# Clamp and low part of the first four weight chunks: from VectorE to Pool

## The chip, the cores and the metric

One Trainium2 chip, one core. The metric is the device time of one execution in microseconds (us). Times of before and after are medians over runs; a profile is one execution. Engines: TensorE is PE in the tables, VectorE is DVE, ScalarE is ACT, GpSimd is Pool; SP issues the DMAs.

## What is computed

An attention whose mask lets a query see the keys of its own cluster, then two layers of a feed-forward kind, each over 1536 tokens with d_model 512 and d_ff 2048:

```python
def _attn_ref(q, k, v, centroids):        # 2 x 8 heads, S = 768, D = 64
    q_assign = np.argmax(q_n . c_n); k_assign = np.argmax(k_n . c_n)
    mask = q_assign[:, :, :, None] == k_assign[:, :, None, :]
    scores = np.where(mask, scale * q @ k.T, -1000000000.0)
    attn = np.exp(scores - max) ; attn = attn / (sum + 1e-09)
    return attn @ v
def _moe_ref(x, w_in, w_out):
    h = x @ w_in
    g = h * np.cos(h)
    return (g @ w_out).astype(np.float32)
def _moe2_ref(x, w_in, w_out):
    h = x @ w_in
    g = np.where(h >= 1, h, np.where(h <= -1, 0.0, (h + 1) ** 2 / 4))
    return (g @ w_out).astype(np.float32)
```

(The lines of the attention are shortened; `...n` are normalised vectors.) The weights of the two layers lie in memory as 64-bit floating-point words.

## The kernel before

Matrix products are made of three matmuls each, since an operand is kept as a high part and a low part (names in h and l: xh, xl; gh, gl; phi, plo): high times high, low times high, high times low (lines 734 to 736).

**Weights.** Each layer's weights come in tiles of 512 columns, w_in and w_out by turns, and each tile as two chunks of 128 x 1024 words; 32 chunks in all. `convert_chunk(n)` turns a chunk into high and low part in seven instructions: Abs on ACT (line 144) into the tile wx, clamp on DVE (146), a shift with mask on DVE (148, below: shl), the low word or-ed in on DVE (151), the sign or-ed in on DVE (154, below: the sign step), the high part on Pool (160, hi), the low part on DVE as wx minus hi (163, lo). With hi, SP is told to load the next chunk. There is one wx and one buffer for the raw words, so a chunk's Abs waits for the lo of the chunk before. The code is a generator with six steps for a chunk, and `pump` takes the next step: in the attention at slots 69, 77, and so on up to 189 (one in eight), after that one with each h tile and each y tile of the layers. So chunk 0 has its Abs at slot 69, clamp at 77, shl at 85, lo at 109; chunk 1 its clamp at 125, lo at 157; chunk 2 its clamp at slot 173 and shl at 181; the rest of chunk 2 and chunk 3 come with the first two blocks of the first layer. Chunks 0 and 1 are the first w_in tile (w_0), chunks 2 and 3 the first w_out tile (w_1): the first y tile needs chunk 2 for f 0 and 1, chunk 3 for f 2 and 3.

**Attention.** 192 slots, 24 for a pair of heads. A slot makes scores (PE, lines 514 and 517); DVE takes the row maximum nm (523), ACT the exponential p (532) with its sum; PE turns p over in three transposes into pt (566), ACT copies it to phi (569), DVE makes plo (574); PE multiplies with the values (584, 585). Three buffers hold pt and the like, so a transpose waits until DVE has made the plo of an earlier one. Pool makes den (541) and rb (552), the values' parts (478, 479), th and tl (318, 319), and xt, xh, xl of a finished pair (606, 607, 623, 624).

**First layer.** For a block of 512 tokens and four f, PE makes an h tile of 12 matmuls; ACT rounds it to n (707), DVE reduces to r (708), ACT takes sine (709) and square (710), DVE makes g (713), Pool gh (696), DVE gl (700). Four buffers hold h, so the fifth h tile waits for the g of the first. Then y tiles of 12 matmuls over four f.

**What sets the order.** Slots 18 to 179 are issued under a manual schedule: PE, ACT, DVE and Pool take the instructions in the written order. Outside of it, from slot 180 on and for work that a step of a late slot issues, the framework's scheduler orders each engine.

Of the kernel before, what the change touches and what calls it, by code (L numbers as in the profile page):

```python
# [8 lines left out]
F32 = mybir.dt.float32  # L9
# [5 lines left out]
ALU = mybir.AluOpType  # L15
# [8 lines left out]
HIGH_MIN = 2.0 ** -15  # L24
HIGH_MAX = 122876.0
# [7 lines left out]
def attention_moe_moe(  # L33
# [18 lines left out]
    nc = tc.nc  # L52
# [76 lines left out]
    def issue_chunk(n):  # L129
        if n >= len(wchunks):  # L130
            return
        src, c0, _ = wchunks[n]
        raw = w0pool.tile([P, 2, 512], I64, tag="wraw", bufs=1, name=f"wraw{n}")
        nc.sync.dma_start(raw, src[:, c0:c0 + 2])
        wraw[n] = raw

    def convert_chunk(n):

        _, c0, w = wchunks[n]
        words = wraw.pop(n).bitcast(I32).rearrange("p c (f t) -> p c f t", t=2)  # L140
        low, high = words[:, :, :, 0], words[:, :, :, 1]
        x = w0pool.tile([P, 2, 512], F32, tag="wx", bufs=1, name=f"wx{n}")
        xi = x.bitcast(I32)
        nc.scalar.activation(x, high.bitcast(F32), AF.Abs)  # L144
        yield
        nc.vector.tensor_scalar(x, x, HIGH_MIN, HIGH_MAX, ALU.max, ALU.min)
        yield
        nc.vector.tensor_scalar(xi, xi, 3, 0x3FFFFFFF,
                                ALU.logical_shift_left, ALU.bitwise_and)
        yield  # L150
        nc.vector.scalar_tensor_tensor(xi, low, 29, xi,
                                       ALU.logical_shift_right, ALU.bitwise_or)
        yield
        nc.vector.scalar_tensor_tensor(xi, high, -0x40000000, xi,
                                       ALU.bitwise_and, ALU.bitwise_or)
        if not wslot:
            wslot.append(w0pool.tile([P, 2, 4, 512], F32R, tag="w_0", name="w_0"))
        t = wslot[w % 4]
        hi, lo = t[:, 0, c0:c0 + 2], t[:, 1, c0:c0 + 2]
        nc.gpsimd.tensor_scalar(hi, x, 1.0, 0.0, ALU.mult, ALU.add)  # L160
        issue_chunk(n + 1)
        yield
        nc.vector.tensor_tensor(lo, x, hi.bitcast(F32), ALU.subtract)
        yield

    for l, (wi, wo) in enumerate(((w1_in, w1_out), (w2_in, w2_out))):
# [7 lines left out]
    def weight_steps():  # L174
        for n in range(len(wchunks)):
            for _ in convert_chunk(n):
                yield n
# [646 lines left out]
```

## Time and profile before

| | us |
|---|---|
| median of 3 runs | 796.08 |
| lowest, highest | 795.78, 798.86 |
| profiled execution | 797.14 |
| its span | 795.2 |
| busy: PE, DVE, ACT, Pool | 774.2, 622.7, 404.0, 282.8 |

The profiled execution took 1.94 us more than its span, and 1.06 more than the median. Times in the rows below are counted from the span's start. A row of a timeline is a run of like instructions: start, duration, engine, line, operation, output and inputs, how often; a bracket gives the idle time of the engine before it and what ended it.

### The profile page before, as it was taken

What the parts mean: (1) busy time and instruction counts of PE and PEld (TensorE: products, weight loads), DVE (VectorE), ACT (ScalarE), POOL (GpSimd) and SP (SyncE); (2) the same over time, 40 slices, a digit from 0 to 9 for tenths busy, and PEclk for the clock granted to TensorE, in tenths of its full rate; (3) what the DMA queues carried; (4) which work ended last, traced back from release to release, by engine and by line L of the source; (5) the groups of instructions that cost most, each with busy time, mean ns of one, the idle gap of its engine ahead of it and who ended that gap; (6) DMA issues with size and microseconds to landing.
All of it is one profiled execution on the core that took longest, in us unless ns stands there. A gap on an engine that the chain in (4) does not pass through costs nothing.

```text
span 795.2 us, 11159 instructions
## 1 busy us (share of the span) xinstructions
PE 774.2 (97%) x3964; PEld 652.9 (82%) x3964; DVE 622.7 (78%) x945; ACT 404.0 (51%) x768; POOL 282.8 (36%) x428
## 2 busy tenths in 40 slices
PE   8899999999999999999999999999999999999998
PEld 5789888888888778888888888888788888888886
DVE  6878988989999597777888788898876988755552
ACT  3788888789788565543333434222444333222220
POOL 4358568578554532122222122342231122111110
PEclk9999999999999999999999999999999999999999
DMA  6864654664430111231311213122122122000012
GB/s 160 192 157 120 145 129 99 145 170 107 88 98 1 54 54 53 106 106 53 107 54 58 101 54 106 54 88 72 54 72 88 53 67 93 0 1 1 19 48 92
DMA packets 46390, 65.95 MB, mean 83 GB/s; under 512 B 27904, under 2 KB 30848, under 8 KB 46336
## 3 DMA queue, kind: packets, MB, share of 16 engines
q1 hardware_dynamic: 46192, 65.22, 29.2%
q8 instruction: 31, 0.51, 0.3%
q14 instruction: 23, 0.19, 0.1%
q10 hardware_dynamic: 144, 0.03, 0.0%
HBM read 43.02 MB, written 3.15 MB: 58 GB/s over the span
## 4 chain that ended last, share of the span: by engine, by line
PE 60%; DVE 22%; POOL 5%; ACT 5%; issue 5%; DMA 3%; SPq 0%; DVEq 0%; POOLq 0%; ACTq 0%
PE y L736 7%; PE y L734 7%; PE y L735 7%; PE pt L566 7%; PE h L734 6%; PE h L735 6%; PE h L736 6%; PE s L514 3%; PE s L517 3%; DVE gl L700 3%; PE o L585 2%; PE o L584 2%; POOL gh L696 2%; DVE plo L574 2%; DVE g L713 2%
## 5 line engine op out<-in xcount | busy, mean ns | idle before, releaser
L696 POOL TENSOR_SCALAR gh<-g 128x512 fp32r<-128x512 f32 x96 | 71.4, 745 | 273.3 <-DVE g L727 152.0
L734 PE MATMUL h<-xh,w 128*128 128x512 f32 x384 | 149.7, 390 | 1.3 <-DVE g L713 0.8
L735 PE MATMUL h<-xl,w 128*128 128x512 f32 x384 | 149.5, 389 | 0.0
L736 PE MATMUL h<-xh,w 128*128 128x512 f32 x384 | 149.4, 389 | 0.0
L569 ACT ACTIVATE phi<-pt 128x384 fp32r<-128x384 f32 x192 | 94.4, 495 | 25.5 <-PE pt L566 22.3
L523 DVE TENSOR_REDUCE nm<-s 128x1 f32<-128x768 f32 x96 | 91.2, 950 | 19.7 <-PE s L517 16.9
L566 PE MATMUL pt<-ident,p 128*128 128x128 f32 x576 | 96.7, 276 | 8.3 <-DVE plo L574 7.0
L574 DVE TENSOR_TENSOR plo<-pt,phi 128x384 fp32r<-128x384 f32 x192 | 98.4, 546 | 7.5 <-ACT phi L569 7.3
L723 ACT ACTIVATE p<-h,ones 128x512 f32<-128x512 f32 x48 | 33.1, 690 | 125.9 <-DVE m L722 125.5
L566 PEld LDWEIGHTS pt<-ident,p 128*128 128x128 f32 x576 | 69.8, 140 | 26.3 <-issue 4.9
L532 ACT ACTIVATE p<-s,nm 128x768 f32<-128x768 f32 x96 | 86.6, 902 | 7.7 <-DVE nm L523 6.1
L700 DVE TENSOR_TENSOR gl<-g,gh 128x512 fp32r<-128x512 f32 x96 | 72.4, 754 | 21.1 <-POOL gh L696 15.4
L734 PEld LDWEIGHTS h<-xh,w 128*128 128x128 f32 x384 | 72.1, 188 | 17.1 <-DVE g L713 1.2
L144 ACT ACTIVATE wx<-wraw 128x1024 f32<-128x1024 f32 x32 | 36.4, 1137 | 96.1 <-DMA wraw<-in_moe_w_out_dram 47.4
L735 PEld LDWEIGHTS h<-xl,w 128*128 128x128 f32 x384 | 72.1, 188 | 14.9
L736 PEld LDWEIGHTS h<-xh,w 128*128 128x128 f32 x384 | 72.1, 188 | 14.8
L514 PE MATMUL s<-st,st 128*128 128x384 f32 x192 | 80.2, 418 | 2.6 <-ACT p L532 2.3
L734 PE MATMUL y<-gh,w 128*128 128x512 f32 x192 | 74.8, 390 | 1.6 <-POOL w L160 1.6
L735 PE MATMUL y<-gl,w 128*128 128x512 f32 x192 | 74.7, 389 | 0.0
L734 PE MATMUL y<-w,gh 128*128 128x512 f32 x192 | 74.7, 389 | 0.0
L735 PE MATMUL y<-w,gh 128*128 128x512 f32 x192 | 74.7, 389 | 0.0
L736 PE MATMUL y<-w,gl 128*128 128x512 f32 x192 | 74.7, 389 | 0.0
(129 smaller groups left out, 1548.2 us busy)
## 6 DMA issues: line engine op xcount, KB each, us to landing
wraw<-in_moe_w_in_dram SPq DMA_DIRECT2D x16, 1024.0 KB, 5.1
wraw<-in_moe_w_out_dram SPq DMA_DIRECT2D x16, 1024.0 KB, 4.8
st<-t SPq DMA_DIRECT2D x24, 192.0 KB, 4.2
st<-th SPq DMA_DIRECT2D x9, 384.0 KB, 4.0
st<-tl SPq DMA_DIRECT2D x18, 192.0 KB, 3.9
st<-th SPq DMA_DIRECT2D x18, 192.0 KB, 3.9
nat<-in_q_dram SPq DMA_DIRECT2D x8, 384.0 KB, 4.6
nat<-in_k_dram SPq DMA_DIRECT2D x8, 384.0 KB, 5.1
```

The lines of the kernel that those rows point to most:

```text
L144: nc.scalar.activation(x, high.bitcast(F32), AF.Abs)
L514: nc.tensor.matmul(s[:, step, :HS], qt[:, 0, cols], kt[:, 0, kc], start=True, stop=False)
L523: nc.vector.tensor_reduce(nm, s[:, :, :HS], AX.XY, ALU.max, negate=True)
L532: nc.scalar.activation(p, s[:, :, :HS], AF.Exp, bias=nm, accum_out=dens[u][:, jj, 0:1])
L566: nc.tensor.transpose(ps[:, jj * P:(jj + 1) * P], p[:, kt * P:(kt + 1) * P], ident)
L569: nc.scalar.activation(hi, ps, AF.Copy)
L574: nc.vector.tensor_tensor(lo, ps, hi.bitcast(F32), ALU.subtract)
L696: nc.gpsimd.tensor_scalar(hi, g, 1.0, 0.0, ALU.mult, ALU.add)
L700: nc.vector.tensor_tensor(lo, g, hi.bitcast(F32), ALU.subtract)
L734: nc.tensor.matmul(o, lh, rh, start=first, stop=False)
L735: nc.tensor.matmul(o, lh, rl, start=False, stop=False)
L736: nc.tensor.matmul(o, ll, rh, start=False, stop=last)
```

## The change

In `convert_chunk`, for the chunks 0 to 3 the clamp and the low part are issued on Pool instead of DVE. The other five instructions, the steps and the later 28 chunks are as before.

```diff
@@ -137,13 +137,14 @@
     def convert_chunk(n):
 
         _, c0, w = wchunks[n]
+        engine = nc.gpsimd if n < 4 else nc.vector
         words = wraw.pop(n).bitcast(I32).rearrange("p c (f t) -> p c f t", t=2)
...
-        nc.vector.tensor_scalar(x, x, HIGH_MIN, HIGH_MAX, ALU.max, ALU.min)
+        engine.tensor_scalar(x, x, HIGH_MIN, HIGH_MAX, ALU.max, ALU.min)
...
-        nc.vector.tensor_tensor(lo, x, hi.bitcast(F32), ALU.subtract)
+        engine.tensor_tensor(lo, x, hi.bitcast(F32), ALU.subtract)
         yield
```

From line 138 on the changed kernel's lines are one higher: clamp 147, shl 149, low word 152, sign step 155, hi 161, lo 164, plo 575. For chunks 0 and 1 the written order holds, and Pool has the clamp and lo where their slots stand. From slot 173 on the scheduler's order differs.

DVE round the clamp of chunk 2 (wx2), slots 171 to 175, before; nm90 and nm91 are row maxima, plo28_5 the low part of the last turned tile of unit 28:

```order
L618 TENSOR_TENSOR xt2_6_0_3773<-xt1_6_0_3727,r6_0_3828 128x384 [waits PE_49,Pool_49]
L523 TENSOR_REDUCE nm89_3844<-s89_3819 128x1 [waits PE_49]
L574 TENSOR_TENSOR plo28_3_3840<-pt28_3_3835,phi28_3_3839 128x384 [waits DVE_49,Activation_49]
L574 TENSOR_TENSOR plo28_4_3851<-pt28_4_3846,phi28_4_3850 128x384 [waits DVE_49,Activation_49]
L545 RECIPROCAL den28_3695<-den28_3695 128x3 [waits Pool_49]
L523 TENSOR_REDUCE nm90_3887<-s90_3853 128x1 [waits PE_49]
L146 TENSOR_SCALAR wx2_3740<-wx2_3740 128x1024
L574 TENSOR_TENSOR plo28_5_3873<-pt28_5_3868,phi28_5_3872 128x384 [waits DVE_49,Activation_49]
L574 TENSOR_TENSOR plo29_0_3895<-pt29_0_3890,phi29_0_3894 128x384 [waits DVE_49,Activation_49]
L523 TENSOR_REDUCE nm91_3918<-s91_3897 128x1 [waits PE_49]
L574 TENSOR_TENSOR plo29_1_3912<-pt29_1_3907,phi29_1_3911 128x384 [waits DVE_49,Activation_49]
```

The same place after:

```order
L524 TENSOR_REDUCE nm89_3844<-s89_3819 128x1 [waits PE_49]
L575 TENSOR_TENSOR plo28_3_3840<-pt28_3_3835,phi28_3_3839 128x384 [waits DVE_49,Activation_49]
L575 TENSOR_TENSOR plo28_4_3851<-pt28_4_3846,phi28_4_3850 128x384 [waits DVE_49,Activation_49]
L546 RECIPROCAL den28_3695<-den28_3695 128x3 [waits Pool_49]
L524 TENSOR_REDUCE nm90_3887<-s90_3853 128x1 [waits PE_49]
L575 TENSOR_TENSOR plo28_5_3873<-pt28_5_3868,phi28_5_3872 128x384 [waits DVE_49,Activation_49]
L575 TENSOR_TENSOR plo29_0_3895<-pt29_0_3890,phi29_0_3894 128x384 [waits DVE_49,Activation_49]
L149 TENSOR_SCALAR wx2_3740<-wx2_3740 128x1024 [waits Pool_49]
L524 TENSOR_REDUCE nm91_3918<-s91_3897 128x1 [waits PE_49]
L575 TENSOR_TENSOR plo29_1_3912<-pt29_1_3907,phi29_1_3911 128x384 [waits DVE_49,Activation_49]
```

The clamp is gone from behind nm90, and shl of wx2 stands behind plo29_0, waits for Pool, and has nm91 and plo29_1 behind it.

Pool at the same place, before; xh and xl are the parts of a finished pair's output:

```order
L606 TENSOR_SCALAR xt2_6_1_3879<-xt0_6_1_3633 64x384 [waits Pool_49]
L606 TENSOR_SCALAR xt2_6_1_3879<-xt1_6_1_3833 64x384 [waits Activation_49]
L606 TENSOR_SCALAR xt1_6_1_3833<-xt0_6_1_3633 64x384 [waits Pool_49]
L607 TENSOR_TENSOR xt1_6_1_3833<-xt1_6_1_3833,xt2_6_1_3879 128x384 [waits Pool_49]
L541 TENSOR_SCALAR den29_3796<-den29_3796 128x3 [waits Activation_49]
L552 TENSOR_SCALAR rb7_0_3885<-den28_3695 128x3x64 [waits DVE_49,PE_49]
L606 TENSOR_SCALAR xt2_7_0_4121<-xt0_7_0_3941 64x384 [waits Activation_49,Pool_49]
L623 TENSOR_SCALAR xh_103<-xt2_6_1_3879 128x384 [waits DVE_49,Pool_49]
```

And after:

```order
L607 TENSOR_SCALAR xt2_6_1_3879<-xt0_6_1_3633 64x384 [waits Pool_49]
L607 TENSOR_SCALAR xt2_6_1_3879<-xt1_6_1_3833 64x384 [waits Activation_49]
L607 TENSOR_SCALAR xt1_6_1_3833<-xt0_6_1_3633 64x384 [waits Pool_49]
L608 TENSOR_TENSOR xt1_6_1_3833<-xt1_6_1_3833,xt2_6_1_3879 128x384 [waits Pool_49]
L542 TENSOR_SCALAR den29_3796<-den29_3796 128x3 [waits Activation_49]
L553 TENSOR_SCALAR rb7_0_3885<-den28_3695 128x3x64 [waits DVE_49,PE_49]
L147 TENSOR_SCALAR wx2_3740<-wx2_3740 128x1024
L607 TENSOR_SCALAR xt2_7_0_4121<-xt0_7_0_3941 64x384 [waits Activation_49,Pool_49]
L624 TENSOR_SCALAR xh_103<-xt2_6_1_3879 128x384 [waits DVE_49,Pool_49]
```

The clamp of wx2 stands behind rb7_0, where xt2_7_0 stood.

PE at the first y tiles of the first layer, before; y0_0_0_0 and y0_0_0_1 are the first two of them, and w_1 is the weight tile of chunks 2 and 3:

```order
L734 MATMUL y0_0_0_0_4401<-gh0_0_0_4199,w_1_4193 128x512
L735 MATMUL y0_0_0_0_4401<-gl0_0_0_4200,w_1_4193 128x512
L736 MATMUL y0_0_0_0_4401<-gh0_0_0_4199,w_1_4193 128x512
L734 MATMUL y0_0_0_0_4401<-gh0_0_0_4199,w_1_4193 128x512
L735 MATMUL y0_0_0_0_4401<-gl0_0_0_4200,w_1_4193 128x512
L736 MATMUL y0_0_0_0_4401<-gh0_0_0_4199,w_1_4193 128x512
L734 MATMUL y0_0_0_1_4418<-gh0_0_0_4199,w_1_4193 128x512
L735 MATMUL y0_0_0_1_4418<-gl0_0_0_4200,w_1_4193 128x512
L736 MATMUL y0_0_0_1_4418<-gh0_0_0_4199,w_1_4193 128x512
L734 MATMUL y0_0_0_1_4418<-gh0_0_0_4199,w_1_4193 128x512
L735 MATMUL y0_0_0_1_4418<-gl0_0_0_4200,w_1_4193 128x512
L734 MATMUL y0_0_0_0_4401<-gh0_0_0_4199,w_1_4193 128x512
```

And after:

```order
L735 MATMUL y0_0_0_0_4401<-gh0_0_0_4199,w_1_4193 128x512
L736 MATMUL y0_0_0_0_4401<-gl0_0_0_4200,w_1_4193 128x512
L737 MATMUL y0_0_0_0_4401<-gh0_0_0_4199,w_1_4193 128x512
L735 MATMUL y0_0_0_0_4401<-gh0_0_0_4199,w_1_4193 128x512
L736 MATMUL y0_0_0_0_4401<-gl0_0_0_4200,w_1_4193 128x512
L737 MATMUL y0_0_0_0_4401<-gh0_0_0_4199,w_1_4193 128x512
L735 MATMUL y0_0_0_0_4401<-gh0_0_0_4199,w_1_4193 128x512
L736 MATMUL y0_0_0_0_4401<-gl0_0_0_4200,w_1_4193 128x512
L737 MATMUL y0_0_0_0_4401<-gh0_0_0_4199,w_1_4193 128x512
L735 MATMUL y0_0_0_0_4401<-gh0_0_0_4199,w_1_4193 128x512
L736 MATMUL y0_0_0_0_4401<-gl0_0_0_4200,w_1_4193 128x512
```

Before, the first six matmuls of y0_0_0_0 (f 0 and 1, chunk 2) are followed by five of y0_0_0_1, and the twelfth is the first that reads chunk 3. After, y0_0_0_0 goes through: its seventh matmul reads the high part of chunk 3, its ninth the low part. On DVE, in this layer, the sign step of chunk 3 stood behind the sixth r, the low word, both g, one gl and the seventh r; after, it stands right behind the sixth r, and the low word ahead of the third gl. On Pool lo of chunk 2 stands behind its hi and ahead of the first gh, the clamp of chunk 3 behind the first gh, its hi behind the fourth gh, and its lo behind the fifth. On ACT the first sine stands ahead of the second n, and the first square behind it; the Abs of chunk 3 stands behind the second sine, where it stood behind the second square and the third n. From about 545 us of the trace of before on, all orders are the same again.

## Rows read from the trace of the kernel before

**Rows 1.** The page: busy us and count by engine; chain's shares; the group of line 144.

```profile
PE 774.2 (97%) x3964; PEld 652.9 (82%) x3964; DVE 622.7 (78%) x945; ACT 404.0 (51%) x768; POOL 282.8 (36%) x428
...
PE 60%; DVE 22%; POOL 5%; ACT 5%; issue 5%; DMA 3%; SPq 0%; DVEq 0%; POOLq 0%; ACTq 0%
...
L144 ACT ACTIVATE wx<-wraw 128x1024 f32<-128x1024 f32 x32 | 36.4, 1137 | 96.1 <-DMA wraw<-in_moe_w_out_dram 47.4
```

**Rows 2.** Windows: from:to, length, busy us (count) of PE, PEld, DVE, ACT, Pool; clock, DMA.

```profile
170.00:250.00 80.00, 76.02 (x506) 68.83 (x506) 73.48 (x130) 67.92 (x150) 49.84 (x79) 1.00 0.42 104
...
300.00:560.00 260.00, 260.00 (x1149) 215.36 (x1148) 210.32 (x276) 100.19 (x156) 64.97 (x75) 1.00 0.23 77
```

**Rows 3.** Waits of PE, whole span: who for whom, us in total, times, longest.

```profile
PE pt L566 <- DVE plo L574: 7.0, 23, 0.8
```

**Rows 4.** Timeline of PE, at the gaps that the prediction names: start, us, instruction, [idle before].

```profile
168.59 0.52 PE L566 MATMUL pt<-ident,p 128*128 128x128 f32 x3 [0.71 <-DVE plo L574]
...
229.56 0.52 PE L566 MATMUL pt<-ident,p 128*128 128x128 f32 x3 [0.84 <-DVE plo L574]
...
249.75 0.52 PE L566 MATMUL pt<-ident,p 128*128 128x128 f32 x3 [0.24 <-DVE plo L574]
...
277.19 0.50 PE L734 MATMUL h<-xh,w 128*128 128x512 f32 x1 [0.77 <-DVE g L713]
...
290.48 0.39 PE L735 MATMUL y<-gl,w 128*128 128x512 f32 x1
...
292.47 0.50 PE L734 MATMUL y<-gh,w 128*128 128x512 f32 x1 [1.60 <-POOL w L160]
```

**Rows 5.** Groups of Pool by line and shape: busy us, mean ns, idle before.

```profile
L160 POOL TENSOR_SCALAR w<-wx 128x1024 fp32r<-128x1024 f32 x32 | 35.1, 1097 | 95.2 <-DVE wx L154 95.2
...
L607 POOL TENSOR_TENSOR xt<-xt,xt 128x384 f32<-128x384 f32 x16 | 16.5, 1034 | 1.3
...
L281 POOL TENSOR_TENSOR cn<-cn 64x64 f32<-64x64 f32 x2 | 0.6, 324 | 0.1
```

**Rows 6.** Timeline of DVE, at the conversion steps and their neighbours.

```profile
124.73 0.68 DVE L146 TENSOR_SCALAR wx<-wx 128x1024 f32<-128x1024 f32 x1
...
135.12 0.90 DVE L148 TENSOR_SCALAR wx<-wx 128x1024 int32<-128x1024 int32 x1
...
166.63 1.34 DVE L163 TENSOR_TENSOR w<-wx,w 128x1024 fp32r<-128x1024 f32 x1
...
246.40 0.95 DVE L146 TENSOR_SCALAR wx<-wx 128x1024 f32<-128x1024 f32 x1
...
247.27 0.54 DVE L574 TENSOR_TENSOR plo<-pt,phi 128x384 fp32r<-128x384 f32 x1
...
248.20 0.94 DVE L523 TENSOR_REDUCE nm<-s 128x1 f32<-128x768 f32 x1
...
276.45 0.69 DVE L713 SCALAR_TENSOR_TENSOR g<-r,h 128x512 f32<-128x512 f32 x1 [1.05 <-ACT r L710]
...
286.66 0.68 DVE L713 SCALAR_TENSOR_TENSOR g<-r,h 128x512 f32<-128x512 f32 x1
...
289.70 1.21 DVE L154 SCALAR_TENSOR_TENSOR wx<-wraw,wx 128x1024 int32<-128x1024 int32 x1
```

**Rows 7.** Timeline of Pool, in the attention part.

```profile
166.99 1.85 POOL L319 TENSOR_TENSOR tl<-t,th 128x384 fp32r<-128x384 f32 x1
...
176.96 1.01 POOL L457 TENSOR_TENSOR eq<-eq,desc 128x384 f32<-128x384 f32 x1 [3.54 <-PE s L517]
...
231.85 0.20 POOL L541 TENSOR_SCALAR den<-den 128x3 f32<-128x3 f32 x1 [3.97 <-ACT p L532]
...
243.41 0.52 POOL L623 TENSOR_SCALAR xh<-xt 128x384 fp32r<-128x384 f32 x1 [3.52 <-DVE xt L618]
...
246.89 1.33 POOL L607 TENSOR_TENSOR xt<-xt,xt 128x384 f32<-128x384 f32 x1
...
248.58 0.35 POOL L552 TENSOR_SCALAR rb<-den 128x192 f32<-128x192 f32 x1
```

## The prediction

> **What bounds the kernel now.** I read the busy shares first, then the windows by stage, the waits of PE, the timelines of PE round each gap, and last VectorE (DVE) and Pool beside these gaps. PE is busy 97% of the span [rows 1] and runs at full granted clock in the windows that matter, so only time in which PE stands still can be won. From 300 to 560 us PE is busy for all of the 260 us [rows 2]; what the change does to DVE and Pool there can only cost. It can win in two places. In the attention part DVE is the next limit: 73.48 of the 80 us between 170 and 250 [rows 2], and PE waits 23 times for plo of DVE, 7.0 us in all [rows 3]. At the start of the first MoE layer PE waits 0.77 us for g and 1.60 us for the high part of chunk 3 [rows 4]. Of the 7.0 us three gaps of PE lie right behind a conversion step that the change moves: 0.71 us at 168.59, 0.84 at 229.56 and 0.24 at 249.75 [rows 4]. All gaps that the change can touch sum to 4.2 us, half a per cent of the time.
>
> **The moved operations.** Eight instructions go from DVE to Pool, all 128x1024: four clamps and four subtractions (lo). On DVE they cost 0.68 and 1.34 us [rows 6]. Pool's clamp has the shape and the single tensor input of hi (line 160), which takes 1.10 us in the mean [rows 5]; I take 1.05, and as upper bound the price of a two-input operation, below. Pool never runs a two-input operation of this size. Its two-input forms take 0.324 us on 64x64 and 1.034 on 128x384 [rows 5]: (1.034 − 0.324) / 320 elements = 2.2 ns an element, so 1.034 + 640 × 2.2 ns = 2.4 us for 1024; in proportion it would be 1.034 × 1024 / 384 = 2.76. I take 2.4, the line through both forms. Below both there is little room, since the operation already costs 1.034 at 384.
>
> **Clamps of chunks 0 and 1: nothing.** DVE's clamp at 124.73 is followed by shl only at 135.12 [rows 6]: over 10 us in which Pool can do 1.05. No PE gap follows either clamp in the timeline. Pool's order there is the written one, and what it delays is th and tl of tiles that are needed later. Between 0 and −0.1 each; I take 0.
>
> **Low parts of chunks 0 and 1: −1.55.** DVE's lo at 166.63 (its row stands in [rows 6]; chunk 1's, at 227.56, is the like) is followed by the PE gaps of 0.71 and 0.84 us [rows 4]. Without lo DVE gives plo 1.3 us sooner, which is more than each gap. So both go: −0.71 − 0.84 = −1.55. On Pool, lo ends some 2.4 us after about 171.9 and 227.9; Pool then idled 3.54 us before 176.96 and 3.97 before 231.85 [rows 7], which hides it. The den and rb that chunk 0's lo pushes back are small and are wanted 5 us later or more. A gain could be smaller where ACT is next (then down to 0); it can't exceed the gaps.
>
> **Clamp of chunk 2: +2.15.** Here the order is the framework's, not the written one. Before, DVE did the clamp at 246.40 and shl much later; after, shl stands right behind plo29_0 and waits for Pool, and behind it are nm91, plo29_1 and all that PE needs next (order of DVE, first pair). On Pool the clamp stands behind the chain that began with xh at 243.41 and ended with rb at 248.58 + 0.35 = 248.93 [rows 7] (order of Pool, second pair). Of this chain 0.3 us came in at 246.89, where Pool's two-input step took 1.33 us [rows 7] against a mean of 1.03 [rows 5], beside DVE's clamp, which itself took 0.95 instead of 0.68 [rows 6]; without it the chain ends at 248.6, and the clamp runs from 248.7 to 249.7. DVE, without the clamp, is through nm90, plo28_5 and plo29_0 at 246.40 + 0.93 = 247.3 (their step is 248.20 − 247.27 [rows 6]) and then stands still for 2.4 us. shl takes 0.6 to 0.7 more (0.68 for the clamp of its shape at 124.73 [rows 6]), so nm91 starts at about 250.35 and not at 248.20 [rows 6]: 2.15 later. PE had no reserve: it waited for this plo already, 0.24 us at 249.75 [rows 4]. So PE resumes 2.15 us later, and that is the cost. Bounds: 0, if Pool's chain is 2.4 us sooner than I have it, and +3.5, if the clamp takes 2.4 us.
>
> **Low part of chunk 2, all of chunk 3: 0, between −0.8 and +0.8.** At the start of the MoE layer lo leaves DVE, and ACT's order lets the first sine and square go ahead of the second rounding. g of the first tile, at 276.45 before [rows 6], is then some 0.5 us sooner, and of PE's gap of 0.77 us at 277.19 [rows 4] about 0.5 goes. What follows is decided at y. A matmul's step is 260.00 / 1149 = 0.23 us [rows 2]. Before, PE did 11 matmuls of y, the last at 290.48, and resumed at 292.47 [rows 4]. After, y0_0_0_0 comes in one run (order of PE, third pair), whose ninth matmul needs the low part of chunk 3, so PE stands still after 8. On DVE the sign step of chunk 3 has lost the clamp and stands ahead of the four instructions between 286.66 and 289.70 [rows 6]: 289.70 − 0.5 − 3.04 − 0.6 = 285.6 with DVE unbroken, 286.5 if g of the second tile waits for most of the chunk's Abs on ACT (1.14 us [rows 1]), which I take. From there: 1.2 sign, 1.05 hi, 0.6 gh, 2.4 lo, to 291.8. Before, PE had 8 matmuls behind it when it had 3 × 0.23 = 0.68 fewer than at 292.47, so 291.79 is the like time: no difference. With DVE unbroken it is −0.8; with 2.76 for lo +0.4, and +0.8 if DVE holds it up for another half operation.
>
> First the row: beside DVE's lo at 166.63 Pool's subtraction of 128x384 took 1.85 us [rows 7] and not the 1.03 of the same shape in line 607 [rows 5]. The Trainium skill, "SBUF — State Buffer", section "Who interferes with whom", says that DVE and GpSimd share one pair of ports, that the one who issues first holds it for its whole instruction, and that a DVE instruction with two SBUF inputs is one that takes it. The trace agrees as far as these rows go. By that rule the sum would be higher by one such DVE instruction in Pool's way, and by rows alone it is as given; it is the upper part of rival C.
>
> **Sum.** −1.55 + 2.15 + 0 = +0.6 us. The profiled execution took 797.14 us, so 797.7; it lay 1.06 above the median of the three runs, and on the median the forecast is 796.08 + 0.6 = 796.7 us. About 0.5%, or 4 us, is what a measurement of this kernel can tell from no change, so this counts as no difference.
>
> **Rivals.**
> (B) DVE doesn't wait for the clamp of chunk 2. It needs Pool to reach it at 247.3, as when the chain from 243.41 starts sooner because DVE, freed of two lo, runs ahead. Against it: each link of that chain was back to back. Then only the gains stay, −1.55, perhaps with the 0.24 gap: 794.5.
> (C) Pool's subtraction is the slow one, and the restart of y pays. Place: the ninth matmul of y0_0_0_0, behind hi, gh and lo on Pool. It decides from about 2.4 us for lo on, one for one: at 2.76 it is +0.4, and with DVE in the way for 0.8 us, as at 166.99 (1.85 against 1.03 [rows 5, 7]), +1.2. With the other terms, 796.7 + 0.4 to 796.7 + 1.2, it is 797.1 to 797.9, and up to 798.7 if the clamp of chunk 2 is held by the same 0.8 us. For it: that row. Against it: the other two-input steps of Pool keep near 1.03 in the mean [rows 5]. The case ends 1.0 to 2.6 us above before.
> (D) The moved work changes nothing that PE sees: ACT gives the pace in attention, the gains of 1.55 don't come, and the DVE wait is taken up by PE's waits behind it, which are all short. 796.1, and up to 796.5.
> (E) The whole order of DVE in the first MoE layer is new, and opens PE gaps between 300 and 545 us, where there were none: DVE work there is 210 of 260 us [rows 2], so one gap of a moved step, 1.2 to 2.4 us, is its price: 798 to 799.
>
> **How the numbers follow.** Forecast, 795.9 to 797.4: 0.45. B, 794.0 to 795.5: 0.2. C, 797.4 to 798.7: 0.18. D: 0.07. E: 0.06. What is left, 0.04, lies outside on either side. The range of 794.3 to 799.2 takes in the forecast, D, most of B and of C and E, 8 in 10 or a little more. A faster kernel by over 0.5% (under 792.1) would need all touched gaps gone and more: 0.03. Slower by over 0.5% (over 800.06) needs C and E together or a longer DVE wait: 0.06. Within 0.5%: 0.91.
>
> **What would show it.** In the profile after, PE's gaps at 168.6 and 229.6 are gone. DVE idles some 2.4 us ahead of line 149 near 247.3 with Pool's wx of line 147 as releaser, and PE has a gap of about 2.4 us for plo near 250. Pool's line 164 takes about 2.4 us four times, line 147 about 1.05. PE waits at y for Pool's w of line 164, not 161, and resumes within 0.8 us of before. From 300 us on PE has no new gap. I am wrong if DVE doesn't wait there (B), if line 164 takes 2.8 us or more (C), or if PE waits in the h and y stages behind 300 us (E).

## The result and the profile after

The changed kernel takes 806.24 us in the median of 4 runs (805.93 to 806.67); the kernel before took 796.14 beside it. The ratio is 1.0124, with a 95% interval of 1.0112 to 1.0136: some 10 us slower. The forecast was 796.7, with a range of 794.3 to 799.2; a kernel slower by over 0.5% had a chance of 0.06.

The page of after (busy us and count by engine), against [rows 1]:

```profile
PE 777.6 (97%) x3963; PEld 655.0 (81%) x3964; DVE 617.7 (77%) x937; ACT 402.4 (50%) x768; POOL 303.9 (38%) x436
```

PE's own work grew by 3.4 us though it does the same matmuls; the rest of the loss is idle time. The waits of PE (us in total, times, longest), against [rows 3]:

```profile
PE pt L567 <- DVE plo L575: 10.9, 21, 5.2
...
PE y L737 <- POOL w L164: 2.2, 1, 2.2
...
PE h L735 <- DVE g L714: 1.9, 2, 1.7
```

Before, the waits for plo were 23, none over 0.8 us. Now one of 5.2 us is among 21. The wait for g at h has grown to 1.9, and y waits for the low part of line 164. What Pool does in the moved instructions, by line and shape (busy us, mean ns, idle before), against [rows 5]:

```profile
L161 POOL TENSOR_SCALAR w<-wx 128x1024 fp32r<-128x1024 f32 x32 | 34.7, 1084 | 85.0 <-DVE wx L155 84.9
...
L147 POOL TENSOR_SCALAR wx<-wx 128x1024 f32<-128x1024 f32 x4 | 14.5, 3625 | 0.9 <-ACT wx L145 0.6
...
L164 POOL TENSOR_TENSOR w<-wx,w 128x1024 fp32r<-128x1024 f32 x4 | 9.5, 2385 | 0.1
```

The subtraction takes 2.385 us; the forecast had 2.4. The clamp takes 3.625 us; the forecast had 1.05, from hi, and 2.4 as its upper bound. hi itself is unchanged. Then the timelines of after at chunk 2's clamp, against [rows 4, 6, 7]. Pool:

```profile
246.97 0.35 POOL L553 TENSOR_SCALAR rb<-den 128x192 f32<-128x192 f32 x1
...
247.38 3.62 POOL L147 TENSOR_SCALAR wx<-wx 128x1024 f32<-128x1024 f32 x1
```

DVE at the same time:

```profile
251.03 0.69 DVE L149 TENSOR_SCALAR wx<-wx 128x1024 int32<-128x1024 int32 x1 [4.90 <-POOL wx L147]
...
251.64 0.95 DVE L524 TENSOR_REDUCE nm<-s 128x1 f32<-128x768 f32 x1
...
252.51 1.01 DVE L575 TENSOR_TENSOR plo<-pt,phi 128x384 fp32r<-128x384 f32 x2
```

PE, in front of its longest gap and behind it:

```profile
247.52 0.49 PE L617 MATMUL r<-ident,rb 128*128 128x128 f32 x3
...
253.20 0.87 PE L567 MATMUL pt<-ident,p 128*128 128x128 f32 x3 [5.20 <-DVE plo L575]
...
254.51 0.84 PE L567 MATMUL pt<-ident,p 128*128 128x128 f32 x3
...
258.98 0.49 PE L567 MATMUL pt<-ident,p 128*128 128x128 f32 x3
```

Pool reached the clamp at 247.38 and was done at 251.0. DVE stood still for 4.90 us before shl, then did nm and plo, and PE resumed at 253.20. And then PE was slow: its transposes of three took 0.87 us instead of 0.49 to 0.52. The windows of after (from:to, length, busy us and count of PE, PEld, DVE, ACT, Pool, then clock, DMA) name the cause:

```profile
252.00:254.00 2.00, 0.80 (x4) 0.83 (x5) 1.98 (x4) 1.37 (x3) 0.00 (x0) 0.53 0.00 0
...
254.00:256.00 2.00, 2.00 (x9) 1.90 (x8) 1.25 (x2) 1.04 (x3) 1.68 (x3) 0.50 0.03 8
...
256.00:258.00 2.00, 2.00 (x8) 1.90 (x8) 0.72 (x3) 0.82 (x2) 0.89 (x3) 0.50 0.00 0
...
258.00:260.00 2.00, 2.00 (x11) 1.91 (x11) 1.41 (x2) 0.99 (x3) 0.00 (x0) 0.76 0.00 0
...
260.00:262.00 2.00, 2.00 (x16) 1.94 (x14) 1.76 (x5) 1.61 (x4) 0.35 (x1) 1.00 0.00 0
```

PE had no work between 248.0 and 253.2. Its granted clock fell while it stood still, to 0.50, which is 1.2 GHz of its 2.4, and came back at about 259. The kernel before has 1.00 in every window of this stage.

To see where the time went, the table has the start of the same PE instruction in both traces and the difference:

| PE instruction, place | before | after | late by | gained or lost since the row above |
|---|---|---|---|---|
| pt, behind clamp of chunk 0 | 136.63 | 136.89 | +0.26 | +0.26 |
| pt, behind lo of chunk 0 | 173.54 | 173.07 | −0.47 | −0.73 |
| pt, behind clamp of chunk 1 | 198.95 | 198.66 | −0.29 | +0.18 |
| pt, behind lo of chunk 1 | 239.22 | 237.96 | −1.26 | −0.97 |
| pt, behind clamp of chunk 2 | 249.75 | 253.20 | +3.45 | +4.71 |
| pt, 3.1 us of work later | 252.89 | 258.98 | +6.09 | +2.64 |
| h, fifth tile | 277.19 | 282.82 | +5.63 | −0.46 |
| h, seventh tile | 282.77 | 290.31 | +7.54 | +1.91 |
| y, behind the waits of the first y tile | 297.13 | 305.79 | +8.66 | +1.12 |
| h, start of the second layer | 570.95 | 580.12 | +9.17 | +0.51 |

From there to the end nothing changes: the spans differ by 804.3 − 795.2 = 9.1 us.

### The profile page after: what moved, and what is told of

It reads as the page before. It is cut to its first block, busy times and chain, and to the rows that moved or that the text cites. A ratio compares the mean times of both kernels' runs of the same rounds, so it can differ in the third digit from the quotient of the medians.

```text
span 804.3 us, 11149 instructions
## 1 busy us (share of the span) xinstructions
PE 777.6 (97%) x3963; PEld 655.0 (81%) x3964; DVE 617.7 (77%) x937; ACT 402.4 (50%) x768; POOL 303.9 (38%) x436
## 4 chain that ended last, share of the span: by engine, by line
PE 64%; DVE 19%; POOL 5%; issue 4%; ACT 4%; DMA 2%; DVEq 0%; POOLq 0%; ACTq 0%; SPq 0%
PE y L737 7%; PE y L735 7%; PE y L736 7%; PE pt L567 7%; PE h L735 7%; PE h L737 6%; PE h L736 6%; PE s L515 3%; PE s L518 3%; PE o L586 3%; PE o L585 3%; DVE plo L575 2%; DVE gl L701 2%; POOL gh L697 2%; DMA wraw<-in_moe_w_out_dram 2%
## 5 line engine op out<-in xcount | busy, mean ns | idle before, releaser
L701 DVE TENSOR_TENSOR gl<-g,gh 128x512 fp32r<-128x512 f32 x96 | 74.1, 773 | 21.9 <-POOL gh L697 16.5
L737 PE MATMUL y<-gh,w 128*128 128x512 f32 x192 | 74.8, 390 | 2.2 <-POOL w L164 2.2
L735 PE MATMUL y<-gh,w 128*128 128x512 f32 x192 | 74.8, 390 | 0.0
```

The source lines that it names most:

```text
L701: nc.vector.tensor_tensor(lo, g, hi.bitcast(F32), ALU.subtract)
L735: nc.tensor.matmul(o, lh, rh, start=first, stop=False)
L737: nc.tensor.matmul(o, ll, rh, start=False, stop=last)
```

## Experiments

Theory "operation": it is max and min that are slow on Pool, and nearly all of the loss comes from the clamps of chunks 2 and 3, by the wait of DVE and by PE's clock behind it. Rivals: the place of the instruction (in place, plain f32 output), the new order, and the low parts.

**e1, the same instruction without max and min.** The edit, to the changed kernel:

```diff
-        engine.tensor_scalar(x, x, HIGH_MIN, HIGH_MAX, ALU.max, ALU.min)
+        if n < 4:
+            nc.gpsimd.tensor_scalar(x, x, 1.0, 0.0, ALU.mult, ALU.add)
+        else:
+            nc.vector.tensor_scalar(x, x, HIGH_MIN, HIGH_MAX, ALU.max, ALU.min)
```

> The changed kernel, but on Pool the four moved clamps are a multiplication by 1 and an addition of 0, in place, on the same tile; the bounds of the clamp are left out for chunks 0 to 3, everything else and the order round chunk 2 stay. Theory 'operation' (max and min are what is slow on Pool, not the shape): the four take about 1.05 us each, as hi does, DVE waits about 2 us and not 4.9 for chunk 2, and the time is 796 to 798 us, near the forecast. Theory 'place' (in-place or plain f32 output is slow there): they take 3.6 us and the time stays near 806. Theory 'order' (the new order of the first MoE layer costs, whatever the clamp takes): 1.05 us each but 802 us or more.

Measured: 801.65 us (799.45 to 803.24), ratio 1.0056 (1.0037 to 1.0074). Pool's group of the moved instruction in this kernel:

```profile
L147 POOL TENSOR_SCALAR wx<-wx 128x1024 f32<-128x1024 f32 x4 | 4.2, 1053 | 0.6 <-ACT wx L144 0.6
```

PE's timeline at chunk 2 in it:

```profile
251.17 0.52 PE L569 MATMUL pt<-ident,p 128*128 128x128 f32 x3 [2.50 <-DVE plo L577]
...
254.04 0.84 PE L569 MATMUL pt<-ident,p 128*128 128x128 f32 x3
```

The operation is the price: 1.053 us, as hi, on the same tile in the same place; "place" falls. PE's gap is 2.50 us, which is what the forecast had worked out for a clamp of 1.05. DVE stands still for 2.20 us ahead of shl, where the forecast had 2.4. But the time is 801.65, not 796 to 798, so about half the loss is left, and the expectation missed. The time alone doesn't rule out "order", which had 802 or more; PE's starts do, below. The windows of this kernel behind the gap (clock third from the end) tell a part of what is left:

```profile
252.00:254.00 2.00, 2.00 (x10) 1.95 (x9) 1.92 (x4) 1.77 (x4) 1.71 (x3) 0.58 0.03 8
...
254.00:256.00 2.00, 2.00 (x10) 1.92 (x9) 0.49 (x2) 0.55 (x2) 0.87 (x3) 0.57 0.00 0
...
256.00:258.00 2.00, 2.00 (x16) 1.93 (x15) 1.77 (x5) 1.62 (x4) 0.35 (x1) 1.00 0.00 0
```

The clock fell here too, after a gap of only 2.5 us: the pt of 249.75 is late by 1.43, that of 252.89 by 2.97, and for the 1.54 us between them my sum had no term. Clamps 0 and 1 cost 0.6 and 0.5 (the pt of 136.63 at 137.22, and from −0.14 to +0.37) instead of 0; DVE's shl behind the first took 1.47 us where it took 0.90 before [rows 6], and behind the second 1.48 against 0.91. The timeline of DVE there:

```profile
135.13 1.47 DVE L151 TENSOR_SCALAR wx<-wx 128x1024 int32<-128x1024 int32 x1
```

And of Pool:

```profile
135.05 1.01 POOL L322 TENSOR_TENSOR t<-t,t 128x384 fp32r<-128x384 f32 x1
```

Pool's two-input step began 0.08 us ahead of shl, and shl ended 0.5 us after Pool's step did: it was held for the length of it. The page "SBUF — State Buffer" of the Trainium skill, section "Who interferes with whom", says that where a DVE instruction goes in a mode that uses two pairs of ports, as tensor_scalar can, whoever of DVE and GpSimd issues first holds the shared pair for the whole instruction. These rows agree. So the clamp's own place was free, but it moved Pool's next steps under shl.

From the pt behind the gap to the first y tiles, where DVE, Pool and PE have the new order as in the changed kernel, PE goes from 2.97 to 2.94 us late: the new order costs nothing there, and "order" falls. The last part of e1's excess, 2.94 to 4.66 us late, comes at the start of the second layer, where h waits for ACT (p). There it is one wait of 0.52 us in the kernel before, and three here, of 0.34, 0.25 and 0.76. These are 0.83 us more, so they tell only a part of the 1.72. The wait's size differs from kernel to kernel (0.22 in e2, 0.75 in e8); what sets it was not tried and stays open.

What the forecast had terms for comes in e1 to −1.72 for the two low parts, +2.05 at chunk 2 and −0.03 at the first layer, +0.3 in all against the forecast's +0.6. The three terms that it lacked come to 1.10 + 1.54 + 1.72 = 4.4.

**e2, the low parts alone.**

```diff
-        nc.vector.tensor_tensor(lo, x, hi.bitcast(F32), ALU.subtract)
+        (nc.gpsimd if n < 4 else nc.vector).tensor_tensor(lo, x, hi.bitcast(F32), ALU.subtract)
```

> Only the four low parts go to Pool, the clamps stay on DVE. Theory 'operation' (the clamps carry the whole loss): the PE gaps of 0.71 and 0.84 us behind lo of chunks 0 and 1 go, y may wait some tenths more or less: 794 to 796 us. Rival 'low parts' (Pool's 2.4 us subtraction of chunk 3 and its hold on DVE's gl carry a part of 2 us or more of the loss): 797 us or more.

Measured: 797.79 us, ratio 1.0003 (0.9993 to 1.0013), no difference. By the trace PE is 1.67 us early from chunk 1's lo on, and gives it back at y. PE's timeline there:

```profile
290.76 0.50 PE L734 MATMUL y<-gh,w 128*128 128x512 f32 x1 [1.60 <-POOL w L160]
...
293.21 0.50 PE L736 MATMUL y<-gh,w 128*128 128x512 f32 x1 [1.25 <-POOL w L163]
```

y waits 1.60 us for hi, as before, and then 1.25 more for Pool's lo of chunk 3; PE is 1.71 us early ahead of it and 0.12 behind. So the low parts of chunks 0 and 1 gain, that of chunk 3 costs 1.6, and neither is the loss of 10 us. The profiled execution took 796.50, below the median of the eleven; the trace doesn't show what the seven of 797.61 and more lost besides. The expectation of 794 to 796 had the cost of chunk 3 too low. By its number, 797 or more, the rival holds; but the kernel is level with the one before, so the low parts can't be what costs 10 us.

**e3, the clamps alone.** The same edit on the clamp's line, lo as before.

> Only the four clamps go to Pool, the low parts stay on DVE. Theory 'operation': four clamps of 3.6 us, a DVE wait of about 5 us at chunk 2, half clock of PE behind it, a wait for the clamp of chunk 3; without the 1.7 us that the low parts of chunks 0 and 1 give back, so 806.5 to 808.5 us. Rival 'low parts': 804 us or less.

Measured: 807.78 us, ratio 1.0129 (1.0113 to 1.0144). As "operation" expected: the clamps alone lose as much as the whole change.

**e4, the low parts of chunks 0 and 1 alone.** As the edit of the low parts, with `n < 2`.

> Only the low parts of chunks 0 and 1 go to Pool; nothing else moves. Both theories: the two PE gaps of 0.71 and 0.84 us go and nothing comes in their place, 794.3 to 794.8 us, ratio about 0.998. If ACT is next there, 795.5 to 796.1.

Measured: 795.18 us, ratio 0.9975 (0.9965 to 0.9986). This is faster than both kernels, by 1.8 us on the kernel before in the same comparison (796.99). Both gaps of [rows 4] are gone and PE is 1.65 us early from 239 us to the end of the first layer. The timeline of Pool at chunk 0's lo in this kernel:

```profile
171.95 2.39 POOL L163 TENSOR_TENSOR w<-wx,w 128x1024 fp32r<-128x1024 f32 x1
...
176.37 1.01 POOL L457 TENSOR_TENSOR eq<-eq,desc 128x384 f32<-128x384 f32 x1 [1.32 <-PE s L517]
```

Of Pool's idle time of 3.54 us ahead of eq [rows 7] 1.32 is left: the 2.39 us fit in.

**e5 and e6, the written order at chunk 2.** The manual schedule is drawn out to slot 187, so that shl of chunk 2 comes at slot 181 and not behind plo29_0; in the changed kernel and in the kernel before:

```diff
-        FIXED = range(18, NSLOT - 12)
+        FIXED = range(18, NSLOT - 4)
```

> The changed kernel with the manual schedule drawn out by 8 slots, to slot 187, so that shl of chunk 2 stands on DVE at its own slot 181 and not ahead of nm91. The clamp on Pool is as slow as before (3.6 us). Theory 'pulled-up wait' (the loss at chunk 2 needs the slow clamp and the shl that the scheduler put right behind it, both): no DVE wait near 247, no PE gap of 5 us, no half clock; 799 to 801 us beside e6, if the drawn-out schedule itself costs nothing. Rival 'slow clamp anyway' (Pool's 3.6 us holds den, rb and xt of the attention up as much): PE gaps of 3 us or more remain and the time is 804 us or more.

> The kernel before with the manual schedule drawn out to slot 187 alone: what this does without the change, as the measure for e5. Both theories: 795 to 798 us.

Measured: with the change 799.50 us, ratio 1.0032 (1.0021 to 1.0043); without it 798.59, ratio 1.0014 (1.0005 to 1.0024). Timelines of the first; Pool's clamp:

```profile
247.59 3.63 POOL L146 TENSOR_SCALAR wx<-wx 128x1024 f32<-128x1024 f32 x1
```

DVE's shl:

```profile
254.03 0.74 DVE L148 TENSOR_SCALAR wx<-wx 128x1024 int32<-128x1024 int32 x1
```

The clamp is as slow, 3.63 us, at nearly the same time. shl stands 6.4 us behind the clamp's start and waits for nothing; PE has no gap over 0.2 us from 240 to 255, and the clock stays at 1.00. Against e6 the change now costs 0.9 us, against the kernel before 2.4 (799.50 − 797.14), and not 10. The first of these may be a low figure: in the profiled execution of e6 the clock fell to 0.55 behind its wait at y, which made it some 1.6 us later there, and how many of the other nine had this is not known; e6 came out 0.6 us above what was expected. Rival "slow clamp anyway" falls. By either measure the loss at chunk 2 needs both, the slow clamp and the shl that the scheduler put right behind it. What is left of e5's loss lies at the start of the first layer, where h waits 1.19 and 0.91 us and y 2.16 (PE goes from 1.66 us early to 0.85 late), and at the start of the second (to 1.77 late).

**e7, the clamp of chunk 2 alone**, `n == 2` on the clamp's line.

> Only the clamp of chunk 2 goes to Pool. Theory 'pulled-up wait': a PE gap of about 5 us near 250 and the half clock behind it, about 4.7 + 2.6 us of the loss: 802.5 to 804 us. Rival (the gap is mostly made up in the waits that follow, and the loss lies at chunk 3): 799 us or less.

Measured: 803.92 us, ratio 1.0085 (1.0070 to 1.0100). PE's gap:

```profile
254.38 0.87 PE L566 MATMUL pt<-ident,p 128*128 128x128 f32 x3 [5.17 <-DVE plo L574]
```

It makes PE 4.6 us late, and the work behind it, at a clock of 0.50 from 254 to 258, another 2.4. At the first y tiles PE is 6.77 us late and stays so to the end. Hardly anything is made up, and the rival falls.

**e10, the clamp of chunk 3 alone**, `n == 3`.

> Only the clamp of chunk 3 goes to Pool. Theory 'operation, behind the queue': DVE's shl of chunk 3 stands still until Pool's 3.6 us are over, g of the third tile and with it PE's h and y come later, 1 to 3 us: 798 to 800 us. Rival (the first MoE layer has cover enough, the 2.1 and 1.0 us lost there in the changed kernel come from its other order): within 0.7 us of before.

Measured: 799.70 us, ratio 1.0044 (1.0027 to 1.0060). The timeline of DVE at the layer's start:

```profile
282.71 0.69 DVE L148 TENSOR_SCALAR wx<-wx 128x1024 int32<-128x1024 int32 x1 [1.48 <-POOL wx L146]
```

PE's waits there:

```profile
284.05 0.50 PE L734 MATMUL h<-xh,w 128*128 128x512 f32 x1 [0.87 <-DVE g L713]
...
295.93 0.50 PE L736 MATMUL y<-gh,w 128*128 128x512 f32 x1 [1.62 <-DVE w L163]
```

DVE stands still at shl, g of the third tile comes late, and h waits 0.87 us where it did not wait before. y then waits 1.62 us; PE is 1.9 us late behind it, 1.7 of it since the layer's start, and 2.5 behind the start of the second layer. Rival "cover enough" falls. The two clamps alone, 803.92 − 797.14 = 6.8 us and 799.70 − 796.91 = 2.8 us, come to 9.6 of the 10; what the rest of the change gains and costs nearly cancels.

**e8 and e9, one bound, and one bound with something else.** Chunks 0 and 1 of the kernel before, on Pool; the left-out bounds are named in the expectations.

```diff
+        if n == 0:
+            nc.gpsimd.tensor_scalar(x, x, HIGH_MIN, None, ALU.max)
+        elif n == 1:
+            nc.gpsimd.tensor_scalar(x, x, 1.0, HIGH_MAX, ALU.mult, ALU.min)
```

> The kernel before, but chunk 0's clamp is only the lower bound (one max, no second operation) on Pool and chunk 1's is a multiplication by 1 and then the upper bound (min) on Pool; the other bound is left out in each. It measures one operation by itself. If each of max and min costs the same on top of about 1 us (3.62 - 1.05 = 2.57, half of it 1.3): about 2.3 us each. If one comparison already takes the slow path: 3.6 in both or in one of them.

```diff
+        if n == 0:
+            nc.gpsimd.tensor_scalar(x, x, HIGH_MIN, 0.0, ALU.max, ALU.add)
+        elif n == 1:
+            for half in range(2):
+                nc.gpsimd.tensor_scalar(x[:, half], x[:, half], HIGH_MIN, HIGH_MAX, ALU.max, ALU.min)
```

> The kernel before, but on Pool chunk 0's clamp is max and then an addition of 0 (the upper bound is left out), and chunk 1's is the whole clamp as two instructions of half the size, 128x512. Theory 'one comparison is enough' (a max or min puts the whole instruction on a slow path): max and add takes 3.6 us, as max and min does. Rival 'each comparison has its price' (max alone 2.78, the second operation priced by what it is): about 2.8 to 3.0 us, since an addition is cheap on Pool. The halves: 1.8 us each if the price goes with the elements, 1.9 or more if a fixed part is in it.

Only the durations count here. Pool's groups in e8, where 147 is max alone and 149 multiplication and min:

```profile
L147 POOL TENSOR_SCALAR wx<-wx 128x1024 f32<-128x1024 f32 x1 | 2.8, 2784 | 0.0
...
L149 POOL TENSOR_SCALAR wx<-wx 128x1024 f32<-128x1024 f32 x1 | 3.6, 3642 | 0.1
```

The same in e9, where 147 is max and addition and 150 the whole clamp on half the tile:

```profile
L147 POOL TENSOR_SCALAR wx<-wx 128x1024 f32<-128x1024 f32 x1 | 3.6, 3638 | 0.0
...
L150 POOL TENSOR_SCALAR wx<-wx 128x512 f32<-128x512 f32 x2 | 3.8, 1918 | 0.1
```

max alone takes 2.78 us; with any second operation it is 3.62 to 3.64, be that min or an addition. Multiplication and min is 3.64 as well. Multiplication and addition is 1.05. So one max or min is enough to make the whole instruction slow, and the rival, 2.8 to 3.0 us for max and addition, falls. Two halves take 3.84, so the price goes nearly with the elements: (3.62 − 1.92) / 512 = 3.3 ns for each, with about 0.2 us that does not.

## Why the prediction was wrong

**The step that failed is the price of the clamp.** "Pool's clamp has the shape and the single tensor input of hi", it said, and "I take 1.05, and as upper bound the price of a two-input operation". Shape and inputs were right, the operation was not looked at. In the trace of before Pool does no max and no min, so the price was unknown, and the bound of 2.4 us came from a row of another operation. It is 3.62. With 1.05 the step's own working gave +2.15, and e1 measured +2.05 for it (from −0.62 to +1.43); with 3.62 the same working gives 2.15 + 2.57 = +4.72, and +4.71 was measured. The forecast had DVE waiting there, at this place, behind these instructions.

**A term was missing: PE's clock behind a gap.** It costs 2.64 us in the changed kernel and 1.54 in e1. Nothing in the trace of before shows a fallen clock in this stage, though PE stands still for 1.60 us there once; so I forecast a gap of 2.4 us and did not ask what PE does after it. Even with the clamp at my price (e1) the time was 801.65 and outside my range. The start of the second layer, +0.51 here and +1.72 in e1, had no term either.

**Low parts of chunks 0 and 1**: forecast −1.55, measured −0.73 − 0.97 = −1.70, and −1.8 us in the time of e4. Right, with its mechanism; only "it can't exceed the gaps" was too strict by some 0.15. And 4 us is not the least that can be told from no change: e4's interval of 0.9965 to 0.9986 tells 1.8.

**Clamps of chunks 0 and 1**: forecast 0, measured +0.26 and +0.18. The slack was smaller than the forecast's 10 us, since Pool came to chunk 0's clamp only at 130.41, 4.7 us ahead of shl; it hid the 3.62 us all the same. What was missed is the shl that Pool's moved steps hold (1.13 us here).

**Low part of chunk 2 and all of chunk 3**: forecast 0 ± 0.8, measured −0.46 + 1.91 + 1.12 = +2.6. In e1, with the clamp at 1.05 us, the same stretch comes to −0.03, so here too it is the clamp's price that was wrong. The first part, g sooner, came as worked out (about −0.5). The 1.91 is shl of chunk 3, for which DVE waits 2.50 us behind the 3.63 us clamp, and with it an r and a g. DVE in the changed kernel:

```profile
287.77 0.69 DVE L149 TENSOR_SCALAR wx<-wx 128x1024 int32<-128x1024 int32 x1 [2.50 <-POOL wx L147]
...
288.38 0.68 DVE L709 SCALAR_TENSOR_TENSOR r<-n,h 128x512 f32<-128x512 int32 x1
...
289.58 0.68 DVE L714 SCALAR_TENSOR_TENSOR g<-r,h 128x512 f32<-128x512 f32 x1
```

PE's two waits in this stretch:

```profile
290.31 0.50 PE L735 MATMUL h<-xh,w 128*128 128x512 f32 x1 [1.75 <-DVE g L714]
...
300.44 0.50 PE L737 MATMUL y<-gh,w 128*128 128x512 f32 x1 [2.17 <-POOL w L164]
```

For y the forecast named the wait for the low part of line 164, and it is there, 2.17 us. In this stretch Pool's lo held DVE as well: gl beside it took 2.83 us, where the gl at 293.93 took 0.69. Two gl on DVE's timeline:

```profile
293.93 0.69 DVE L701 TENSOR_TENSOR gl<-g,gh 128x512 fp32r<-128x512 f32 x1
...
298.11 2.83 DVE L701 TENSOR_TENSOR gl<-g,gh 128x512 fp32r<-128x512 f32 x1
```

Pool's lo of chunk 3:

```profile
298.03 2.35 POOL L164 TENSOR_TENSOR w<-wx,w 128x1024 fp32r<-128x1024 f32 x1
```

Here it fell on a gl for which PE did not wait.

**Rivals.** C named the right place for a loss, Pool's queue, and the wrong instruction: not the subtraction (2.39 as forecast) but the clamp, at chunk 2. B, no DVE wait, did not happen, since DVE waited 4.90 us; e4 avoids the wait by leaving the clamps on DVE, and gains 1.8 us where B had 1.55. D falls with e4, where the gains come. E did not happen: from 300 to 560 us PE is busy for 259.56 us, and the 0.44 that is missing lies ahead of 300.44.

## What to carry over

Before an operation moves to another engine, price the operation there, not only its shape: if no row of the trace shows that operation on that engine, the bound has to be wide, and a run that times the operation there, as e1, e8 and e9 do, settles the price. An instruction in front of which a scheduler leaves a wait stops its engine for all that is queued behind it; it was the pulled-up shl that made a hidden 3.6 us into 5.2 us of PE, and behind a gap of PE the half clock has to be in the sum as a possible term, since it came behind some gaps and not behind others. The part of such a change that fills idle time of the other engine may be worth keeping alone, as here the two low parts.

## What was not expected of the hardware

On Pool, a tensor_scalar over 128x1024 f32 takes 1.05 us with multiplication and addition, 2.78 with max alone, and 3.62 to 3.64 with max or min and a second operation; DVE does max and min in 0.68 [rows 6]. The Trainium skill's page "GPSIMD Engine Reference", section "4.1 Engine selection", says of elementwise add, mul and max that one-input operations run at roughly line rate there. The rows agree for multiplication and addition, and don't for max: with max and min the same tile takes 3.4 times as long (min isn't named there). The rows decide. Other one-input operations of this size were not run, so which of them are slow on Pool stays open.

PE's granted clock fell to 0.50 after PE had stood still for 5.2 us, and in e1 after 2.5 us; it did not fall in the changed kernel behind the gaps of 1.75 and 2.17 us, and did in e6 behind one of 1.82. PE's gap in e6:

```profile
292.88 0.50 PE L734 MATMUL y<-gh,w 128*128 128x512 f32 x1 [1.82 <-POOL w L160]
```

And the window behind it, with the clock at 0.55:

```profile
294.00:296.00 2.00, 2.00 (x7) 1.57 (x6) 1.68 (x3) 0.50 (x1) 0.23 (x1) 0.55 0.80 328
```

So the length of the gap alone does not tell. Where it fell behind chunk 2, it cost 2.64 and 1.54 us on top of the gap.
